# Five instead of four wide blocks, unsplit k and q projections, and a later plan for DMA results in a fused attention and feed-forward kernel

## Chip, cores and metric

The kernel runs on one core of one Trainium2 chip. Its time is device time in microseconds (us); 1131.34 us is the median of three runs (1127.63 to 1132.11). TensorE is called PE here, VectorE DVE, ScalarE ACT, GpSimd POOL; SP issues the DMAs.

## What is computed

Eight batches of eight heads, 576 tokens of 64 numbers each, go through a linear attention with a feature map; its output, seen as 4608 tokens of 512 numbers, goes through a two-layer network with a GELU.

```python
def phi(x):                                   # w_phi: 64 x 128
    proj = einsum('bhsd,df->bhsf', x, w_phi)
    proj = proj - max(abs(proj), axis=-1, keepdims=True)
    return concatenate([exp(proj), exp(-proj)], axis=-1)
q_p, k_p = phi(q), phi(k)
kv  = einsum('bhsf,bhsd->bhfd', k_p, v)
z   = sum(k_p, axis=2)
num = einsum('bhsf,bhfd->bhsd', q_p, kv)
den = einsum('bhsf,bhf->bhs', q_p, z)[..., None] + 1e-06
x   = (num / den) as 4608 x 512
h   = x @ w_in                                # 512 x 2048
g   = 0.5 * h * (1 + erf(h / sqrt(2)))
out = g @ w_out                               # 2048 x 512
```

## The kernel before

**Order.** The program does not run in the order in which it is written. Every operation is first recorded with an engine, an assumed cost and a rank (`op`, line 91). `Plan.order` (line 118) then replays all of them: on each engine it takes, among those whose inputs and buffers are there, the one with the lowest rank, and `emit` writes the instructions in the order of the starts found. Each engine then runs its own list strictly in that order, so an instruction that waits holds up all that stand behind it on its engine. The numbers from line 901 on are the planner's settings: `T0`, `T15`, `LEAD`, `ATR`, `TF` and `HOLD2` say when blocks and batches fall due, `WPACE` and `WSPAN` when weights do, `LUMP` and `LINGER` how much attention work is gathered before PE leaves the feed-forward products. What a DMA brings counts as usable at its planned landing (line 243).

**Attention, k side** (`k_quad`, line 395; 16 of them, two a batch). Four heads at a time. Keys `kt` stand with two heads on the two halves of the 128 rows. In nine chunks of 128 tokens they are multiplied by `w_phi` into `pk` (PSUM), DVE takes the absolute maximum `mx` and subtracts it into `ek`, ACT takes the two exponentials, and PE adds up `kv` (with a column of ones for the sums). For batches 0 and 1 (`b < EB`) each chunk is two fp32 products, one on each half of PE's rows. For batches 2 to 7 the way is "full": DVE splits `kt` into `kh` (a CAST to fp32r and a TENSOR_TENSOR for the rest), and three fp32r products with the block-diagonal weight `wbd` (128 x 256, two parts) make both heads at once.

**Attention, q side** (`q_pair`, line 503; 64 of them, a pair of heads and half of the tokens each). For batches 0 and 1 the queries `qt` are loaded with two heads on the row halves and multiplied in fp32, two products side by side. For batches 2 to 7 they are loaded twice over by two DMAs, DVE splits them into `qh` (CAST and TENSOR_TENSOR), and each head takes two fp32r products against `wd`. ACT copies `pq` to `pc`, POOL takes the maximum over partitions (`mb`), DVE subtracts, ACT takes two exponentials into `ef`; PE makes the numerators `pn`; DVE (`un`), POOL (`db`), DMAs through DRAM (`d_d`, `dc`, `r_d`) and a reciprocal on DVE make the quotients.

**Weights** arrive as 64-bit floats and are turned into two fp32r parts on ACT and DVE (`split_weight`, line 346; 32 of them, 5 DVE instructions each).

**Plain blocks** (`block`, line 620): 256 tokens each. DVE multiplies `xr` by the quotients and splits it (`xh`, `xl`). Eight units follow: 24 products of 128x256 into `ph`, two GELUs on ACT, `gl` on DVE, 12 products of 128x512 into `po`. Plain blocks run among the attention work.

**Wide blocks** (`wide_block`, line 718): 512 tokens each, with seven products instead of eight for the first layer (42 products of 128x256 a unit into `pa` and `pb`, 336 a block against 384 for two plain blocks). Their extra weight sums come from `combos` (line 688; `sw`, `sh` on DVE, written to DRAM). They use the buffers of the attention, so they wait for its end. `JW` = 5 makes ten plain blocks (0 to 9) and then four wide ones (5 to 8, counted in 512 tokens).

Of the kernel before, what the change touches and what calls it, by code (L numbers as in the profile page):

```python
# [285 lines left out]
def fused_kernel(ctx: ExitStack, tc: tile.TileContext, qT, kT, va, w_st, w_in, w_out, out):  # L286
# [108 lines left out]
    def k_quad(b, g, kvs, rank):  # L395
# [23 lines left out]
        for u, (p, cs) in enumerate(units):  # L419
# [22 lines left out]
            cols = slice(cs[0] * P, (cs[-1] + 1) * P)  # L442
            if way == "full":
                kh = sb["kh"]([P, 2, n * P], F32R, f"kh_{nm}_{u}")
                copy("dve", dve(n * P, fast=True), lambda kh=kh: kh()[:, 0], lambda cols=cols: kt()[:, cols], [kts[u]], [kh], also=[kt], **k())
# [3 lines left out]
                def proj(xb=xb, cs=cs, kh=kh):
                    ins = []  # L450
                    for i, c in enumerate(cs):
                        at = slice(i * 2 * NF, (i + 1) * 2 * NF)
# [50 lines left out]
    def q_pair(b, p, kvs, rank, halves=(0, 1)):  # L503
# [4 lines left out]
        for half in halves:  # L508
            nm = f"{b}_{p}_{half}"
            ss = slice(half * HS, half * HS + HS)  # L510
            qt = sb[("qt", "gh", "gl")[(2 * p + half) % 3] if b < EB else "qt"]([P, HS] if b < EB else [P, 2, HS], F32, f"qt_{nm}")
            if b < EB:
                op("sp", 0.06, lambda qt=qt, ss=ss: nc.sync.dma_start(out=qt(), in_=qT[b, p, :, ss]), w=[qt], kb=147, **k(1))
            else:
# [15 lines left out]
            if b < EB:  # L530
                op("pe", PAIR_Q, lambda of=of, qt=qt: [
                    mm(of[j](), lhsT=wst()[64 * j : 64 * j + 64], rhs=qt()[64 * j : 64 * j + 64], start=True, stop=True) for j in range(2)
                ], r=[qt, wst], w=pqs, also=[pc], kind="q", **k(1))
            else:
                for j in range(2):
# [444 lines left out]
```

## Time and profile before

| | |
|---|---|
| median of three runs | 1131.34 us |
| the profiled execution | 1126.56 us |
| its span, first to last instruction | 1124.8 us |
| PE busy | 1080.4 us (96%) |
| DVE busy | 760.1 us (68%) |
| ACT busy | 620.0 us (55%) |
| POOL busy | 328.2 us (29%) |
| mean granted TensorE clock | 0.993 |

The busy shares are means over stages that differ. A matmul is shown longer than the step to the next one, since matmuls overlap in the array: what one costs in a row of them is the difference of two starts. The rows below give the stages, the waits of PE and the costs of the single steps.

### The profile page before, as it was taken

How to read it: one execution, taken by the hardware profiler on the slowest of the kernel's cores; microseconds unless marked ns; L12 is line 12 of the kernel's file. 1: busy time of each engine (PE TensorE's matmuls, PEld its weight loads, DVE VectorE, ACT ScalarE, POOL GpSimd, SP SyncE). 2: the span in 40 equal slices, each digit the busy share in tenths (PEclk: the TensorE clock that was granted, in tenths of full speed). 3: DMA queues.
4: the chain of work that ended last, by engine and by line, in shares of the span. 5: the costliest groups of instructions: out<-in, count | busy, mean ns of one | idle time of the engine just before them, and what ended most of it. 6: DMA issues, size and time to landing. Idle time of an engine off the chain costs nothing.

```text
span 1124.8 us, 22298 instructions
## 1 busy us (share of the span) xinstructions
PE 1080.4 (96%) x8796; PEld 913.5 (81%) x8796; DVE 760.1 (68%) x1352; ACT 620.0 (55%) x1063; POOL 328.2 (29%) x116
## 2 busy tenths in 40 slices
PE   7887999998998999999999999999999999999998
PEld 5544887886887888888888888999898898888987
DVE  6998999678887999987778887223535535534332
ACT  5886786777776778778777643122223223222222
POOL 2153024445565656555466342000000000000000
PEclk9989999999999999999999999999999999999999
DMA  9965232333342342341322345502635534523421
GB/s 352 339 230 142 63 95 74 88 98 92 89 115 73 91 137 56 95 135 51 109 80 59 105 137 164 150 20 58 186 104 139 171 102 142 160 85 123 131 85 38
DMA packets 119480, 133.98 MB, mean 119 GB/s; under 512 B 28544, under 2 KB 88096, under 8 KB 119376
## 3 DMA queue, kind: packets, MB, share of 16 engines
q1 hardware_dynamic: 119376, 132.56, 39.6%
q8 instruction: 69, 1.13, 0.4%
q14 instruction: 35, 0.29, 0.1%
HBM read 104.96 MB, written 27.56 MB: 118 GB/s over the span
## 4 chain that ended last, share of the span: by engine, by line
PE 59%; DVE 21%; DMA 6%; ACT 4%; issue 4%; POOL 3%; SPq 2%; ACTq 0%; DVEq 0%; POOLq 0%
PE po L305 25%; PE ph L305 10%; PE pb L305 8%; PE pa L305 5%; PE pn L305 4%; PE kv L305 3%; POOL db L576 2%; PE pk L305 2%; DVE qh L331 2%; DVE pc L331 2%; PE pq L305 2%; DMA dc<-d_d 1%; DVE mx L469 1%; DVE qh L327 1%; DVE gl L331 1%
## 5 line engine op out<-in xcount | busy, mean ns | idle before, releaser
L305 PE MATMUL po<-w_o,gh 128*128 128x512 f32 x1152 | 362.1, 395 | 0.0
L305 PE MATMUL ph<-xh,w_i 128*128 128x256 f32 x1280 | 246.0, 281 | 1.5 <-DVE gl L331 1.5
L305 PEld LDWEIGHTS po<-w_o,gh 128*128 128x128 f32 x1152 | 205.6, 188 | 37.3 <-issue 0.4
L576 POOL PARTITION_ALL_REDUCE db<-un x48 | 178.3, 3714 | 178.5 <-DVE un L573 127.6
L305 PE MATMUL po<-w_o,gl 128*128 128x512 f32 x576 | 227.1, 394 | 0.0
L305 PEld LDWEIGHTS ph<-xh,w_i 128*128 128x128 f32 x1280 | 204.5, 188 | 5.9 <-issue 1.8
L541 POOL PARTITION_ALL_REDUCE mb<-pc x64 | 152.4, 2383 | 193.7 <-ACT pc L325 159.6
L305 PE MATMUL ph<-xl,w_i 128*128 128x256 f32 x640 | 181.0, 283 | 0.1
L305 PEld LDWEIGHTS po<-w_o,gl 128*128 128x128 f32 x576 | 108.3, 188 | 26.3 <-DVE gl L331 0.4
L305 PEld LDWEIGHTS ph<-xl,w_i 128*128 128x128 f32 x640 | 120.3, 188 | 2.2 <-DVE xl L331 0.4
L834 ACT ACTIVATE gh<-pa 128x512 fp32r<-128x512 f32 x32 | 19.2, 600 | 174.1 <-PE po L305 120.2
L305 PE MATMUL pn<-ef,kvn 128*64 128x288 f32 (+1 forms) x512 | 97.9, 423 | 10.8 <-ACT ef L547 7.4
L305 PEld LDWEIGHTS kv<-vt,ek 128*64 128x64 f32 (+1 forms) x2560 | 84.6, 139 | 28.8 <-issue 12.8
L547 ACT ACTIVATE ef<-pc 128x576 f32<-128x576 f32 x128 | 82.8, 679 | 29.9 <-DVE pc L331 29.2
L305 PE MATMUL kv<-vt,ek 128*64 128x65 f32 (+1 forms) x2560 | 94.0, 226 | 4.6 <-ACT ek L477 3.8
L477 ACT ACTIVATE ek<-ek 128x512 f32<-128x512 f32 (+1 forms) x140 | 82.0, 587 | 21.2 <-DVE ek L331 18.7
L331 DVE TENSOR_TENSOR gl<-ph,gh 128x512 fp32r<-128x512 f32 x80 | 54.9, 686 | 56.2 <-ACT ph L664 54.4
L663 ACT ACTIVATE gh<-ph 128x512 fp32r<-128x512 f32 x80 | 47.8, 598 | 80.7 <-PE ph L305 78.1
L305 PE MATMUL pb<-b,s 128*128 128x256 f32 x576 | 78.9, 282 | 1.0 <-DVE c L331 1.0
L305 PEld LDWEIGHTS pn<-ef,kvn 128*64 128x64 f32 (+1 forms) x512 | 38.8, 138 | 45.6 <-ACT ef L547 12.5
L305 PEld LDWEIGHTS pb<-b,s 128*128 128x128 f32 x576 | 73.0, 189 | 2.2 <-DVE c L331 1.6
L663 ACT ACT_TABLE_LOAD x57 | 73.1, 1283 | 1.9 <-PE ph L305 1.0
(84 smaller groups left out, 1558.3 us busy)
## 6 DMA issues: line engine op xcount, KB each, us to landing
s<-s_d SPq DMA_DIRECT2D x128, 256.0 KB
qt<-in_qT_dram SPq DMA_DIRECT2D x112, 144.0 KB
kt<-in_kT_dram SPq DMA_DIRECT2D x16, 576.0 KB
out_dram<-ob SPq DMA_DIRECT2D x36, 256.0 KB
raw_i<-in_w_in_dram SPq DMA_DIRECT2D x16, 512.0 KB
raw_o<-in_w_out_dram SPq DMA_DIRECT2D x16, 512.0 KB
x_d<-xo SPq DMA_DIRECT2D x48, 144.0 KB
vt<-in_va_dram SPq DMA_DIRECT2D x16, 325.0 KB
```

What stands on the lines that cost most here:

```text
L305: return tc.keep_in_program_order(nc.tensor.matmul(*a, **kw))
L327: op(eng, cost, lambda: e.tensor_copy(out=dst(), in_=src()), r=r, w=w, **kw)
L331: op(eng, cost, lambda: e.tensor_tensor(out=dst(), in0=a(), in1=b(), op=o), r=r, w=w, **kw)
L469: op("dve", dve(128 * n * nj, True), lambda view=view, mx=mx, js=js: nc.vector.tensor_reduce(out=mx()[:, 0].rearrange("p (j i) -> p j i", ...
L477: op("act", act(256 * n, inside), lambda at=at, es=es, s=s: nc.scalar.activation(es[s](), at(), AF.Exp, scale=1.0 - 2.0 * s), r=[parts[0][ ...
L541: op("pool", 2.2, lambda mb=mb, pc=pc: nc.gpsimd.partition_all_reduce(mb(), pc(), P, bass_isa.ReduceOp.absmax), r=[pc], w=[mb], **k(1))
L547: op("act", act(2 * HS), lambda ef=ef, pc=pc, s=s: nc.scalar.activation(ef()[:, s], pc(), AF.Exp, scale=1.0 - 2.0 * s), r=[pc], w=[ef], ta ...
L576: op("pool", 3.7, lambda db=db, un=un: nc.gpsimd.partition_all_reduce(db(), un(), P, bass_isa.ReduceOp.add), r=[un], w=[db], **k())
L663: op("act", act(2 * TB, True) + 0.016, lambda gh=gh, ph=ph: nc.scalar.activation(gh(), ph(), AF.Gelu), r=[ph], w=[gh], table="gelu", rank= ...
L834: op("act", act(2 * TB, psum) + 0.016, lambda gh=gh, at=at: nc.scalar.activation(gh(), at(), AF.Gelu), r=[at], w=[gh], table="gelu", rank= ...
```

## The change

One more pair of plain blocks becomes a wide one (`JW` = 4: plain blocks 0 to 7, wide blocks 4 to 8). For batches 2 to 7 the splits on DVE go. k is one unsplit fp32 product a chunk with an fp32 block-diagonal weight; q takes the way that batches 0 and 1 had, with one DMA instead of two. `wd` and `kh` are gone. A result of a DMA that another engine than PE reads is planned as there 4 us later (`LANDING`). The planner's settings are new.

```diff
+                u.ready = max(u.ready, ... 
+                              + (LANDING if o.eng == "sp" != u.eng and u.eng != "pe" and o.end > 130.0 else 0.0))
...
-    copy("dve", dve(NF), lambda: wd()[:, 0], wst, [wst], [wd], rank=-100.0)
-    tt("dve", dve(NF), lambda: wd()[:, 1], wst, lambda: wd()[:, 0].bitcast(F32), ALU.subtract, [wst, wd], [wd], rank=-100.0)
...
-    wbd = fixed([P, 2, 2 * NF], F32R, "wbd")
+    wbd = fixed([P, 2 * NF], F32, "wbd")
...
             if way == "full":
-                kh = sb["kh"]([P, 2, n * P], F32R, f"kh_{nm}_{u}")
-                copy("dve", dve(n * P, fast=True), lambda kh=kh: kh()[:, 0], lambda cols=cols: kt()[:, cols], [kts[u]], [kh], also=[kt], **k())
-                tt("dve", dve(n * P), lambda kh=kh: kh()[:, 1], lambda cols=cols: kt()[:, cols], lambda kh=kh: kh()[:, 0].bitcast(F32), ALU.subtract,
-                   [kts[u], kh], [kh], also=[kt], **k())
...
-                        for z, w in ((0, 0), (0, 1), (1, 0)):
-                            ins.append(mm(xb[0]()[:, at], lhsT=kh()[:, z, i * P : (i + 1) * P],
-                                          rhs=wbd()[:, w], start=len(ins) % 3 == 0, stop=len(ins) % 3 == 2))
...
+                    return [mm(xb[0]()[:, i * 2 * NF : (i + 1) * 2 * NF], lhsT=kt()[:, c * P : (c + 1) * P], rhs=wbd(), start=True, stop=True)
+                            for i, c in enumerate(cs)]
...
-                for i in range(2):
-                    op("sp", 0.06, lambda qt=qt, ss=ss, i=i: nc.sync.dma_start(
-                        out=qt()[64 * i : 64 * i + 64], in_=qT[b, p, :, ss].rearrange("(j d) t -> d j t", j=2)), w=[qt], kb=147, **k(1))
-                qh = sb["mb"]([P, 2, HS], F32R, f"qh_{nm}")
-                copy("dve", dve(2 * HS, fast=True), qh, qt, [qt], [qh], **k(1))
-                tt("dve", dve(2 * HS), lambda qh=qh: qh()[64:], lambda qt=qt: qt()[64:], lambda qh=qh: qh()[64:].bitcast(F32), ALU.subtract,
...
-                    op("pe", 2 * mm_cost(128, HS), lambda of=of, qh=qh, j=j: [
-                        mm(of[j](), lhsT=wd()[:, w], rhs=qh()[:, j], start=w == 0, stop=w == 1) for w in range(2)
-                    ], r=[qh, wd], w=[pqs[j]], also=[pc], kind="s", **k(1))
+            op("pe", PAIR_Q, lambda of=of, qt=qt: [
+                mm(of[j](), lhsT=wst()[64 * j : 64 * j + 64], rhs=qt()[64 * j : 64 * j + 64], start=True, stop=True) for j in range(2)
+            ], r=[qt, wst], w=pqs, also=[pc], kind="q", **k(1))
...
-JW = 5
+JW = 4
+LANDING = 4.0
-HOLD2 = 12.718
+HOLD2 = 73.438
-TF = 83.043
+TF = 65.043
-LUMP = 2.465
+LUMP = 1.394
-WPACE = 2.116
-WSPAN = 4.373
+WPACE = 2.884
+WSPAN = 12.477
-LEAD = 289.427
+LEAD = 316.642
-T0 = 76.06
+T0 = 83.683
```

DVE, ahead of the first plain block (`xl_0` is the last thing its first product needs; `wt` and `w` are weights). Before, at the place of `xl_0`; its partner `xh_0` stands 23 rows above it:

```order
L331 TENSOR_TENSOR w_i0_2_1437<-wt_i0_2_1348,w_i0_2_1437 128x512
L362 SCALAR_TENSOR_TENSOR wt_i1_2_1396<-raw_i1_2_509,wt_i1_2_1396 128x512
L331 TENSOR_TENSOR pc_1_3_1_1418<-pc_1_3_1_1418,mb_1_3_1_1435 128x576
L356 TENSOR_SCALAR wt_i2_2_1456<-wt_i2_2_1456 128x512
L331 TENSOR_TENSOR kh_2_0_1_1430<-kt_2_0_772,kh_2_0_1_1430 128x256
L331 TENSOR_TENSOR w_i1_2_1465<-wt_i1_2_1396,w_i1_2_1465 128x512
L358 TENSOR_SCALAR wt_i2_2_1456<-wt_i2_2_1456 128x512
L331 TENSOR_TENSOR xl_0_1485<-xr_0_1189,xh_0_1331 128x1024
```

And now:

```order
L330 TENSOR_TENSOR pc_1_3_0_1355<-pc_1_3_0_1355,mb_1_3_0_1372 128x576
L348 TENSOR_SCALAR wt_i0_2_1384<-wt_i0_2_1384 128x512
L326 CAST xh_0_1424<-xr_0_938 128x1024
L350 TENSOR_SCALAR wt_i0_2_1384<-wt_i0_2_1384 128x512
L330 TENSOR_TENSOR xl_0_1434<-xr_0_938,xh_0_1424 128x1024
L330 TENSOR_TENSOR w_o7_1436<-wt_o7_1300,w_o7_1436 128x512
```

`xl_0` has moved up to `xh_0`: work on weights `i0_2`, `i1_2` and `i2_2` that stood ahead of it stands behind it.

PE, in batch 4 (`pq_4_0_1` is the second half of its first pair of heads). Before, the two heads stand apart among products of plain block 3:

```order
L305 MATMUL ph_3_2_4287<-xh_3_3027,w_i3_1_1030 128x256
L305 MATMUL pq_4_0_1_0_4339<-qh_4_0_1_4300,wd_95 128x288 x2
L305 MATMUL po_3_4241<-w_o2_692,gh_3_1_4249 128x512 x2
L305 MATMUL po_3_4241<-w_o2_692,gl_3_1_4266 128x512
L305 MATMUL po_3_4241<-w_o2_692,gh_3_1_4249 128x512 x2
L305 MATMUL po_3_4241<-w_o2_692,gl_3_1_4266 128x512
L305 MATMUL pq_4_0_1_1_4355<-qh_4_0_1_4300,wd_95 128x288 x2
```

And now:

```order
L306 MATMUL ph_2_3_3688<-xh_2_2405,w_i3_1_1084 128x256
L306 MATMUL pk_4_1_2_3750<-wbd_80,kt_4_1_3115 128x256
L306 MATMUL pn_3_3_1_3754<-ef_3_3_1_3685,kvn_3_1_1_3200 64x288 x4
L306 MATMUL pq_4_0_1_0_3768<-qt_4_0_1_3719,wst_68 128x288
L306 MATMUL pq_4_0_1_1_3770<-qt_4_0_1_3719,wst_68 128x288
L306 MATMUL kv_4_1_0_3710<-vt_4_1_0_3528,ek_4_1_1_0_3701 64x65 x2
```

The two heads read `qt` as it was loaded, run side by side, and stand in one lump with other attention products; the block whose products stand around batch 4 is 2 instead of 3.

DVE, where the k side of batch 4 begins. Before:

```order
L327 CAST kh_4_0_0_3693<-kt_4_0_3025 128x256
L573 SCALAR_TENSOR_TENSOR un_3_1_1_3680<-ef_3_1_1_3567,kvn_3_0_1_3180,un_3_1_1_3680 128x288
L331 TENSOR_TENSOR kh_4_0_0_3693<-kt_4_0_3025,kh_4_0_0_3693 128x256
L573 SCALAR_TENSOR_TENSOR un_3_1_1_3680<-ef_3_1_1_3567,kvn_3_0_1_3180,un_3_1_1_3680 128x288
L327 CAST qh_3_2_1_3716<-qt_3_2_1_3613 128x576
L331 TENSOR_TENSOR qh_3_2_1_3716<-qt_3_2_1_3613,qh_3_2_1_3716 64x576
L469 TENSOR_REDUCE mx_4_0_0_3766<-pk_4_0_0_3749 128x4
L327 CAST kh_4_0_1_3782<-kt_4_0_3025 128x256
L331 TENSOR_TENSOR ek_4_0_0_0_3784<-pk_4_0_0_3749,mx_4_0_0_3766 128x512
L331 TENSOR_TENSOR kh_4_0_1_3782<-kt_4_0_3025,kh_4_0_1_3782 128x256
```

And now:

```order
L330 TENSOR_TENSOR gl_1_6_3088<-ph_1_6_3010,gh_1_6_3056 128x512
L451 TENSOR_REDUCE mx_3_1_4_3113<-pk_3_1_4_3107 128x4
L330 TENSOR_TENSOR ek_3_1_4_0_3128<-pk_3_1_4_3107,mx_3_1_4_3113 128x512
L451 TENSOR_REDUCE mx_4_0_0_3130<-pk_4_0_0_3110 128x4
L537 TENSOR_SCALAR un_3_0_1_3134<-ef_3_0_1_3105,kvn_3_0_0_2549 128x288
L330 TENSOR_TENSOR ek_4_0_0_0_3143<-pk_4_0_0_3110,mx_4_0_0_3130 128x512
```

The splits `kh` and `qh` are gone, and the maxima of batch 4 stand in plain block 1.

## Rows read from the trace of the kernel before

**Rows 1.** Stages: stretch, length, busy PE, PEld, DVE, ACT, POOL; clock, DMA share, GB/s.
```profile
0.00:115.20 115.20, 95.80 (x1024) 57.39 (x1025) 97.68 (x187) 84.86 (x184) 37.49 (x20) 0.94 0.77 260
115.20:697.70 582.50, 566.43 (x5170) 482.76 (x5168) 497.52 (x838) 423.64 (x673) 287.83 (x96) 1.00 0.34 95
697.70:768.60 70.90, 70.90 (x449) 63.58 (x446) 17.95 (x30) 14.91 (x28) 2.91 (x1) 1.00 0.30 82
768.60:1124.80 356.20, 347.25 (x2161) 309.73 (x2159) 146.96 (x298) 96.61 (x180) 0.00 (x0) 1.00 0.40 120
```

**Rows 2.** Waits of PE, 115.2 to 697.7 us: total us, times, longest.
```profile
PE pq L305 <- DVE qh L331: 8.5, 11, 1.5
PE pq L305 <- DVE ek L331: 2.6, 4, 1.6
...
PE ph L305 <- DVE gl L331: 1.5, 1, 1.5
```

**Rows 3.** PE in order of time: start us, us, instructions, [idle before <-releaser].
```profile
344.54 0.50 PE L305 MATMUL pq<-qh,wd 128*128 128x288 f32 x2 [1.54 <-DVE qh L331]
...
354.14 0.43 PE L305 MATMUL pq<-qh,wd 128*128 128x288 f32 x2
354.41 0.28 PE L305 MATMUL ph<-xh,w_i 128*128 128x256 f32 x1
```

**Rows 4.** DVE in order of time, at the same place.
```profile
343.43 0.18 DVE L596 TENSOR_SCALAR dc<-dc 128x18 f32<-128x18 f32 x1 [3.43 <-DMA dc<-d_d]
343.64 0.76 DVE L331 TENSOR_TENSOR qh<-qt,qh 64x576 fp32r<-64x576 f32 x1
```

**Rows 5.** Instructions by form, DVE: count, busy us, mean ns, idle before.
```profile
L331 DVE TENSOR_TENSOR qh<-qt,qh 64x576 fp32r<-64x576 f32 x48 | 49.0, 1022 | 1.6
L327 DVE CAST qh<-qt 128x576 fp32r<-128x576 f32 x48 | 41.4, 863 | 7.1 <-DMA qt<-in_qT_dram 5.7 <-PE ph L305 1.0 <-issue 0.3
L331 DVE TENSOR_TENSOR kh<-kt,kh 128x256 fp32r<-128x256 f32 x48 | 29.7, 619 | 0.4
L327 DVE CAST kh<-kt 128x256 fp32r<-128x256 f32 x48 | 24.6, 512 | 1.1 <-PE pk L305 1.0
```

**Rows 6.** PE in order of time, a k unit of two chunks and a kv group.
```profile
482.33 0.87 PE L305 MATMUL pk<-wbd,kh 128*128 128x256 f32 x6
483.03 0.27 PE L305 MATMUL ph<-xh,w_i 128*128 128x256 f32 x1
...
484.31 0.28 PE L305 MATMUL ph<-xh,w_i 128*128 128x256 f32 x1
484.52 0.68 PE L305 MATMUL kv<-vt,ek 64*64 64x65 f32 x16
```

**Rows 7.** PE in order of time, fp32 products of batches 0 and 1.
```profile
79.88 0.76 PE L305 MATMUL pq<-qt,wst 64*128 64x288 f32 x4
80.56 1.19 PE L305 MATMUL pn<-ef,kvn 128*65 128x288 f32 x4
81.68 0.68 PE L305 MATMUL kv<-vt,ek 64*64 64x65 f32 x16
```

**Rows 8.** Chain that ended last: start us, us, what; one unit of a plain block.
```profile
701.08 2.83 PE ph L305 x24
703.91 2.80 PE po L305 x12
```

**Rows 9.** PE in order of time, the last attention product and the first wide block's first.
```profile
696.89 1.19 PE L305 MATMUL pn<-ef,kvn 128*64 128x288 f32 x8
...
768.56 1.59 PE L305 MATMUL pb<-b,s 128*128 128x256 f32 x12
...
1120.01 0.40 PE L305 MATMUL po<-w_o,gl 128*128 128x512 f32 x1
```

**Rows 10.** DVE in order of time, ahead of the first plain block.
```profile
98.28 0.69 DVE L327 CAST xh<-xr 128x1024 fp32r<-128x1024 f32 x1
...
114.53 1.22 DVE L331 TENSOR_TENSOR xl<-xr,xh 128x1024 fp32r<-128x1024 f32 x1
```

More of the change, by code (lines that the diff above doesn't have):

```diff
@@ L242, in order @@
                 u.wait -= 1
-                u.ready = max(u.ready, o.end + o.late + (self.HOP if u.eng != o.eng else self.SAME)[o.eng] + (MARGIN if u.eng == "pe" != o.eng and o.end > 130.0 else 0.0))
+                u.ready = max(u.ready, o.end + o.late + (self.HOP if u.eng != o.eng else self.SAME)[o.eng] + (MARGIN if u.eng == "pe" != o.eng and o.end > 130.0 else 0.0)
+                              + (LANDING if o.eng == "sp" != u.eng and u.eng != "pe" and o.end > 130.0 else 0.0))
                 if u.wait == 0:
@@ L318, in fused_kernel @@
     op("sp", 0.06, lambda: nc.sync.dma_start(out=wst(), in_=w_st), w=[wst], kb=66, rank=-400.0)
-    wd = fixed([P, 2, NF], F32R, "wd")
     def copy(eng, cost, dst, src, r, w, **kw):
@@ L331, in tt @@
         op(eng, cost, lambda: e.tensor_tensor(out=dst(), in0=a(), in1=b(), op=o), r=r, w=w, **kw)
-    copy("dve", dve(NF), lambda: wd()[:, 0], wst, [wst], [wd], rank=-100.0)
-    tt("dve", dve(NF), lambda: wd()[:, 1], wst, lambda: wd()[:, 0].bitcast(F32), ALU.subtract, [wst, wd], [wd], rank=-100.0)
-    wbd = fixed([P, 2, 2 * NF], F32R, "wbd")
-    op("dve", dve(512, fast=True), lambda: nc.vector.memset(wbd().bitcast(F32), 0.0), w=[wbd], rank=WB)
+    wbd = fixed([P, 2 * NF], F32, "wbd")
+    op("dve", dve(2 * NF, fast=True), lambda: nc.vector.memset(wbd(), 0.0), w=[wbd], rank=WB)
     for j in range(2):
-        copy("dve", dve(2 * NF, fast=True), lambda j=j: wbd()[64 * j : 64 * j + 64, :, j * NF : (j + 1) * NF], lambda j=j: wd()[64 * j : 64 * j + 64],
-             [wd, wbd], [wbd], rank=WB)
+        copy("dve", dve(NF, fast=True), lambda j=j: wbd()[64 * j : 64 * j + 64, j * NF : (j + 1) * NF], lambda j=j: wst()[64 * j : 64 * j + 64],
+             [wst, wbd], [wbd], rank=WB)
     def split_weight(src, nm, rank):
@@ L441, in k_quad, with proj @@
             turn[0] += 1
-            cols = slice(cs[0] * P, (cs[-1] + 1) * P)
             if way == "full":
-                kh = sb["kh"]([P, 2, n * P], F32R, f"kh_{nm}_{u}")
-                copy("dve", dve(n * P, fast=True), lambda kh=kh: kh()[:, 0], lambda cols=cols: kt()[:, cols], [kts[u]], [kh], also=[kt], **k())
-                tt("dve", dve(n * P), lambda kh=kh: kh()[:, 1], lambda cols=cols: kt()[:, cols], lambda kh=kh: kh()[:, 0].bitcast(F32), ALU.subtract,
-                   [kts[u], kh], [kh], also=[kt], **k())
[L449 to L452, printed above, removed]
-                        for z, w in ((0, 0), (0, 1), (1, 0)):
-                            ins.append(mm(xb[0]()[:, at], lhsT=kh()[:, z, i * P : (i + 1) * P],
-                                          rhs=wbd()[:, w], start=len(ins) % 3 == 0, stop=len(ins) % 3 == 2))
-                    return ins
-                op("pe", 3 * n * mm_cost(128, 2 * NF), proj, r=[kh, wbd], w=xb, also=[mx, *e], kind="s", **k())
+                def proj(xb=xb, cs=cs):
+                    return [mm(xb[0]()[:, i * 2 * NF : (i + 1) * 2 * NF], lhsT=kt()[:, c * P : (c + 1) * P], rhs=wbd(), start=True, stop=True)
+                            for i, c in enumerate(cs)]
+                op("pe", n * FULL_K, proj, r=[kts[u], wbd], w=xb, also=[kt, mx, *e], kind="s", **k())
             else:
@@ L510, in q_pair @@
             ss = slice(half * HS, half * HS + HS)
[L511 to L514, printed above, removed]
-                for i in range(2):
-                    op("sp", 0.06, lambda qt=qt, ss=ss, i=i: nc.sync.dma_start(
-                        out=qt()[64 * i : 64 * i + 64], in_=qT[b, p, :, ss].rearrange("(j d) t -> d j t", j=2)), w=[qt], kb=147, **k(1))
-                qh = sb["mb"]([P, 2, HS], F32R, f"qh_{nm}")
-                copy("dve", dve(2 * HS, fast=True), qh, qt, [qt], [qh], **k(1))
-                tt("dve", dve(2 * HS), lambda qh=qh: qh()[64:], lambda qt=qt: qt()[64:], lambda qh=qh: qh()[64:].bitcast(F32), ALU.subtract,
-                   [qt, qh], [qh], **k(1))
+            qt = sb[("qt", "gh", "gl")[(2 * p + half) % 3] if b < EB else "qt"]([P, HS], F32, f"qt_{nm}")
+            op("sp", 0.06, lambda qt=qt, ss=ss: nc.sync.dma_start(out=qt(), in_=qT[b, p, :, ss]), w=[qt], kb=147, **k(1))
             pc = sb["pc"]([P, 2, HS], F32, f"pc_{nm}")
@@ L529, in q_pair @@
                 of = [lambda t=t: t() for t in pqs]
[L530 to L535, printed above, removed]
-                    op("pe", 2 * mm_cost(128, HS), lambda of=of, qh=qh, j=j: [
-                        mm(of[j](), lhsT=wd()[:, w], rhs=qh()[:, j], start=w == 0, stop=w == 1) for w in range(2)
-                    ], r=[qh, wd], w=[pqs[j]], also=[pc], kind="s", **k(1))
+            op("pe", PAIR_Q, lambda of=of, qt=qt: [
+                mm(of[j](), lhsT=wst()[64 * j : 64 * j + 64], rhs=qt()[64 * j : 64 * j + 64], start=True, stop=True) for j in range(2)
+            ], r=[qt, wst], w=pqs, also=[pc], kind="q", **k(1))
             for j in range(2):
@@ L909 @@
 GATE = 60
-T15 = 906.055
+T15 = 901.177
 BIAS = 40
 STICK = 2
-PATIENCE = 1.567
+PATIENCE = 0.947
 URGE = -1000.0
-EARLY = -18.706
-WPACE = 2.116
-WSPAN = 4.373
+EARLY = -26.856
+WPACE = 2.884
+WSPAN = 12.477
 WARM = 4
@@ L926 @@
 EPACE = 20.0
-TF = 83.043
+TF = 65.043
 ND = 2
-LUMP = 2.465
-LINGER = 3.999
+LUMP = 1.394
+LINGER = 4.006
 PAIR_K = 0.43
-PAIR_Q = 0.7
+FULL_K = 0.433
+PAIR_Q = 0.5
 PAIR_N = 1.18
@@ L935 @@
 PULL = -2000.0
-LEAD = 289.427
-HOLD = 44.655
-WR = -30.275
-ATR = -8.845
-T0 = 76.06
+LEAD = 316.642
+HOLD = 89.189
+WR = -14.66
+ATR = 9.181
+T0 = 83.683
 VERBOSE = False
```

2 lines of the change are left out of this document (1 added, 1 removed).

## Prediction

> **What bounds the kernel now.** I read the stages first [rows 1]. Up to 115.2 us PE is not the bound: it is busy for 95.8 us, with matmuls that are shown longer than the step they take, at a mean clock of 0.94 of 2.4 GHz, while DVE has 97.7 us of work. From 115.2 to 697.7 us, ten plain blocks and the attention of batches 2 to 7 share PE, which is idle for 16.1 of 582.5 us; but DVE is busy for 497.5 us (85%), ACT for 423.6 (73%), POOL for 287.8 (49%). Then come 71 us of plain blocks alone without a gap, and four wide blocks in 356.2 us, with DVE at 41%. So PE bounds all but the start, and what it loses in the middle is short waits. Who ends them [rows 2]: 8.5 us for the split queries `qh`, 2.6 us for `ek`, 1.5 us for a `gl`, all on DVE. One such place shows the mechanism: PE stands 1.54 us before `pq` [rows 3]; the subtraction that makes `qh` started only at 343.64 because the instruction ahead of it on DVE stood 3.43 us for the quotients' DMA [rows 4]. A shown wait hides some more, since a matmul is shown for 0.28 us or longer where the next follows after 0.12 [rows 3, 8]; with 0.16 us for each of some 20 waits, about 16 us are lost in this stage to DVE or through it.
>
> **Part 1, k without a split.** A unit of two chunks takes 0.70 us as six fp32r products (482.33 to 483.03), 0.35 a chunk [rows 6]. Now a chunk is one fp32 product of 128 rows by 256 columns. The trace of before has this only as `pn` of batches 0 and 1: two fp32 products of 288 columns in 1.12 us (80.56 to 81.68) [rows 7], so 0.56 each, and 0.50 if scaled to 256 columns. In that time lies a change of tile shape; one such change costs about 0.09 us on leaving (`ph` at 484.31 is followed after 0.21 instead of 0.12) [rows 6], and with some on entering I take off 0.13 for the two products: 0.44 a chunk. There are 12 quads of nine chunks: 108 x (0.44 - 0.35) = +9 us on PE. Bounds: +16 without taking anything off, +3 if a chunk in a lump with other attention work already costs 0.41 today, as 0.35 plus half a change.
>
> **Part 2, q on row halves.** So far a head is two fp32r products, 0.27 us (354.14 to 354.41) [rows 3], so 0.54 for a pair of heads. The pair in fp32 on the two halves takes 0.68 us from its start to that of the next group (79.88 to 80.56) [rows 7], with the change of shape behind it. That is +0.14 us, and up to 0.10 more where the change into it comes on top: 48 x 0.14 to 0.24 = +7 to +11.5. In the new order PE changes its tile shape 177 instead of 117 times behind the first `ph`, so the changes are not all shared; but most pairs stand beside `kv` or `pn`, which change the shape anyway. I take +8. The Trainium skill speaks against this part: "TensorEngine Tiling (Array Packing)", Key Properties, says that a change of tiling mode drains TensorE; the rows agree with about 0.1 us a change. The same page's table promises up to twice the speed for a contraction of 64; by that the pair would cost 0.27 us and the part would give 13 us back, which the 0.68 us of the row rule out here.
>
> **Part 3, the fifth wide block.** A unit of a plain block takes 2.83 + 2.80 us [rows 8], two blocks 90.1. Four wide blocks run from 768.56 to 1120.4 [rows 9], 88.0 each with their gaps. So -2 us; by the count alone, 48 products of 2.83/24 = 0.118 us fewer, it would be -5.7, the far bound.
>
> **Part 4, the waits.** `kh` and `qh` cost DVE 49.0 + 41.4 + 29.7 + 24.6 = 144.7 us [rows 5], more with the ninth chunks. The stage in the middle shrinks by two plain blocks, to some 490 us plus what parts 1 and 2 add; DVE then has at most 353 us of work in it, 72% or less. The split's own wait (8.5 us, and 11 times the hidden 0.16) goes entirely, since `qt` is now read as it lands; its DMA was loaded far ahead and, with one instead of two for each pair, stays so. Of the rest, planning DMA results 4 us later puts other work ahead of an instruction such as the one at 343.43, so I let half of it go. What is late next is the PSUM buffer of `pq`, freed by ACT and DVE. Sum: -14 of 16; bounds 0 and -18.
>
> **Part 5, the start.** The first plain product comes at 115.2, straight behind `xl` at 114.53, which stood 23 instructions behind `xh` at 98.28 [rows 10]. In the new order `xl` follows `xh` after one instruction. Counted with the mean duration of each form, 92.5 instead of 100.4 us of DVE work then stand up to and including `xl`, and PE has no less attention work before its first plain product. So -8 us; bounds -10 and 0, since weights are released more slowly and DVE could wait for their DMAs.
>
> **Free edits.** The three small instructions for `wd` (0.9 us) lie in the start beside DMAs. 48 DMA issues fewer for `qt` against 32 more for the sums of one more wide block: SP is never waited for in rows that end a PE wait.
>
> **Sum.** +9 + 8 - 2 - 14 - 8 = -7 us, and from about -24 to +26 if every part fell to the same end of its bounds. The profiled execution took 1126.56 us, 4.8 us less than the median of the runs shown; a change of some us is taken over unscaled, so the median should go from 1131.3 to about 1124.
>
> **Rivals.**
> (a) *Slower: ACT takes DVE's place.* ACT's work in the middle hardly shrinks (the attention's copies and exponentials stay), while the stage does: up to 424 us in 490, 86%, against 73%, and ACT also runs its list in order. If PE then waits for the copies of `pq` and for the GELUs as it did for DVE, part 4 gives nothing and the sum is +9 + 8 - 2 - 8 = +7; with the dearer q it is +11: 1138 to 1142. It decides when the average wait on ACT per q pair reaches 0.3 us (48 x 0.3 = 14 us). For it: [rows 1]. Against it: ACT ends almost none of PE's waits now, and PE's own work in the stage also falls more slowly than its length, so it stays the fullest.
> (b) *No change: gains and costs meet.* Half of the waits stay, or the first wide block comes late. Behind the last attention product there are now less than seven units of plain work, 6.9 x 5.63 = 39 us instead of 71 [rows 9], for the attention's last results to pass through DRAM and DVE to make the wide block's seven operands. Either costs some 6 us: 1127 to 1134.
> (c) *A larger gain.* Part 1 at its low bound, part 3 by the count, waits all gone: -7 - 6 - 4 - 4 = -21: about 1110.
> (d) *The change does not do what it says.* The later planned landing holds only for the planner; if the real landings are not what held DVE up, only the removed splits act: the half of "the rest" in part 4, 3 us, stays out: 1127.
>
> **How the numbers follow.** The forecast, 1124 us, has 0.45; (a) 0.18; (b) and (d) together 0.25; (c) 0.12. A measurement of this kernel can tell about 0.5% (5.7 us) from no change. The forecast's own spread, some 5 us either way, lies a little more than half on the faster side of 1125.7: 0.32 faster, 0.13 same. With (c) and a part of (b) and (d): faster 0.50; same 0.31; slower 0.19, from (a) and the edge of (b). The range reaches from (c) to (a), with a little beyond each: 1108 to 1141.
>
> **What would show it.** Right: no `pq` waits for DVE; a lower DVE share in the middle; the first plain product near 107 us; the unit of k at 0.85 to 0.95 us; the wide stage 88 us longer. Part 4 is wrong if PE's waits in the middle still come to over 10 us, and (a) is right if ACT ends them. Part 5 is wrong if the first product stays at 115. I am wrong altogether if the fp32 products cost PE much more than rows 7 suggest, or if PE waits over 5 us at the first wide block.

## The result and the profile after

The changed kernel takes 1112.75 us (median of four runs, 1111.32 to 1114.11) against 1130.38 for the kernel before on the same chip: ratio 0.985, 95% interval 0.982 to 0.987, so 17.6 us faster where 7 were forecast. One execution of all those below, one of run e12, took 2095.92 us and is left out of its median. The profiled execution took 1112.2 us with a span of 1110.4. These are its stages, to be read against [rows 1]; columns as there.

```profile
0.00:107.80 107.80, 93.36 (x1046) 59.68 (x1046) 90.10 (x175) 81.83 (x177) 33.55 (x19) 0.95 0.85 275
107.80:643.20 535.40, 530.23 (x4701) 429.49 (x4702) 356.68 (x617) 400.14 (x646) 284.29 (x97) 1.00 0.31 87
643.20:677.40 34.20, 34.20 (x221) 30.74 (x218) 11.92 (x22) 6.92 (x13) 0.00 (x0) 1.00 0.46 137
677.40:1110.40 433.00, 428.84 (x2678) 384.28 (x2676) 187.47 (x379) 120.62 (x224) 0.00 (x0) 1.00 0.42 126
```

In the second row DVE has fallen from 85% to 67% of the stage, ACT stands at 75%, and PE is idle for 5.2 us instead of 16.1. The longest waits of PE in this stage, against [rows 2] (total us, times, longest); none is for `qh`, and ACT ends most of what is left:

```profile
PE pk L306 <- ACT pc L324: 1.6, 3, 1.1
PE pq L306 <- DVE ek L330: 1.3, 1, 1.3
PE pn L306 <- ACT xo L324: 1.2, 3, 0.8
```

By three marks of the trace (first plain product, first wide product, end of the last product) the span divides so: up to the first mark 107.8 us instead of 115.2, -7.4; between the marks 569.6 instead of 653.4, which with the 90.1 us of two plain blocks fewer is +6.3; wide blocks 428.8 us for five instead of 351.8 for four, and +77.0 against 90.1 is -13.1. The forecast had -8, +3 and -2. The start and the middle came out near it, the middle in part by luck (see Part 4 below). The wide blocks did not, and they say where to look: in the kernel before they had waits of which the prediction showed no row.

```profile
DVE xr L331 <- DMA rp<-r_d: 19.1, 9, 4.3
...
PE pa L305 <- DVE u L331: 3.6, 3, 1.4
PE pb L305 <- DVE c L331: 1.0, 2, 0.6
```

These are waits of the kernel before, 768.6 to 1124.8 us. One of them in order of time, on DVE and then on PE (start us, us, instruction, [idle before <-releaser]):

```profile
879.52 0.68 DVE L331 TENSOR_TENSOR gl<-pa,gh 128x512 fp32r<-128x512 f32 x1
882.36 0.69 DVE L331 TENSOR_TENSOR xr<-xr,rp 128x512 f32<-128x512 f32 x1 [2.15 <-DMA rp<-r_d]
882.97 0.42 DVE L327 CAST b<-xr 128x512 fp32r<-128x512 f32 x1
883.31 0.69 DVE L331 TENSOR_TENSOR gl<-c,gh 128x512 fp32r<-128x512 f32 x1
883.91 0.41 DVE L331 TENSOR_TENSOR u<-u,pa 128x256 f32<-128x256 f32 x1
...
884.38 0.97 PE L305 MATMUL pa<-b,w_i 128*128 128x256 f32 x6 [0.89 <-DVE u L331]
```

DVE stands 2.15 us for the quotients `rp` of the *next* wide block. Behind that one instruction wait `gl` and `u` of the block that runs, and PE waits for `u`. After, again inside the second wide block, while the operands of the third are made, the multiplications stand further back, and the long wait is gone; the stage's total is 3.1 us in four waits, and PE shows none:

```profile
786.39 0.42 DVE L330 TENSOR_TENSOR u<-u,pa 128x256 f32<-128x256 f32 x1
786.73 0.69 DVE L330 TENSOR_TENSOR xr<-xr,rp 128x512 f32<-128x512 f32 x1
787.42 0.42 DVE L330 TENSOR_TENSOR u<-u,pb 128x256 f32<-128x256 f32 x1
...
788.75 0.69 DVE L330 TENSOR_TENSOR xr<-xr,rp 128x512 f32<-128x512 f32 x1 [0.45 <-DMA rp<-r_d]
...
DVE xr L330 <- DMA rp<-r_d: 3.1, 4, 1.4
```

### The profile page after: what moved, and what is told of

Same layout as the page of the kernel before. It is cut to its first block, busy times and chain, and to the rows that moved or that the text cites. A ratio compares the mean times of both kernels' runs of the same rounds, so it can differ in the third digit from the quotient of the medians.

```text
span 1110.4 us, 21848 instructions
## 1 busy us (share of the span) xinstructions
PE 1086.6 (98%) x8640; PEld 904.2 (81%) x8640; DVE 646.2 (58%) x1190; ACT 609.5 (55%) x1059; POOL 317.8 (29%) x116
## 4 chain that ended last, share of the span: by engine, by line
PE 79%; DVE 7%; ACT 5%; DMA 3%; issue 3%; POOL 1%; SPq 1%; ACTq 0%; DVEq 0%; POOLq 0%
PE po L306 33%; PE ph L306 13%; PE pb L306 10%; PE pa L306 8%; PE kv L306 5%; PE pn L306 4%; PE pk L306 4%; PE pq L306 3%; DMA raw_i<-in_w_in_dram 2%; POOL mb L508 1%; ACT L630 1%; ACT ek L459 1%; DVE mx L451 1%; ACT ef L514 1%; DVE ek L330 1%
## 5 line engine op out<-in xcount | busy, mean ns | idle before, releaser
L306 PE MATMUL ph<-xh,w_i 128*128 128x256 f32 x1024 | 201.6, 285 | 0.0
L306 PEld LDWEIGHTS ph<-xh,w_i 128*128 128x128 f32 x1024 | 165.0, 189 | 7.5 <-issue 3.9
L306 PE MATMUL ph<-xl,w_i 128*128 128x256 f32 x512 | 145.4, 284 | 0.0
L306 PEld LDWEIGHTS ph<-xl,w_i 128*128 128x128 f32 x512 | 96.9, 189 | 2.8
L306 PE MATMUL pb<-b,s 128*128 128x256 f32 x720 | 98.4, 282 | 0.0
L451 DVE TENSOR_REDUCE mx<-pk 128x4 f32<-128x512 f32 (+2 forms) x90 | 51.6, 577 | 73.6 <-PE pk L306 73.6
L306 PEld LDWEIGHTS pb<-b,s 128*128 128x128 f32 x720 | 91.5, 189 | 0.8
L330 DVE TENSOR_TENSOR gl<-ph,gh 128x512 fp32r<-128x512 f32 x64 | 44.0, 688 | 67.8 <-ACT ph L631 62.7
L306 PEld LDWEIGHTS pa<-b,w_i 128*128 128x128 f32 x480 | 67.4, 188 | 7.1
L537 DVE TENSOR_SCALAR un<-ef,kvn 128x288 f32<-128x288 f32 x96 | 49.5, 534 | 39.7 <-POOL db L543 37.0
```

The source lines that it names most:

```text
L306: return tc.keep_in_program_order(nc.tensor.matmul(*a, **kw))
L330: op(eng, cost, lambda: e.tensor_tensor(out=dst(), in0=a(), in1=b(), op=o), r=r, w=w, **kw)
L451: op("dve", dve(128 * n * nj, True), lambda view=view, mx=mx, js=js: nc.vector.tensor_reduce(out=mx()[:, 0].rearrange("p (j i) -> p j i", ...
L537: op("dve", dve(HS, fast=True) + 0.06, lambda un=un, ef=ef, one=one, j=j: nc.vector.tensor_scalar(out=un()[:, j], in0=ef()[:, 0, j], scala ...
```

## The experiments

The first theory was that the later plan (`LANDING`) took these waits out and that the rest came out about as forecast. Its rivals were the new settings and the fifth wide block. The table holds all runs, by what they are; the marks are us in each profiled span, the ratio is to the kernel before on the same chip.

| label | kernel | median us | ratio, 95% interval | first plain | first wide | last product ends |
|---|---|---|---|---|---|---|
| | before | 1130.38 | 1 | 115.2 | 768.6 | 1120.4 |
| | after | 1112.75 | 0.982 to 0.987 | 107.8 | 677.4 | 1106.2 |
| e2 | before, landing 4 | 1104.62 | 0.974 to 0.981 | 114.5 | 754.1 | 1098.7 |
| e11 | before, landing 4 in wide blocks only | 1121.18 | 0.990 to 0.995 | 113.8 | 769.4 | 1115.2 |
| e9 | e2, k unsplit | 1117.41 | 0.987 to 0.992 | 117.7 | 767.7 | 1113.6 |
| e10 | e2, q unsplit | 1114.22 | 0.983 to 0.989 | 111.5 | 761.0 | 1106.8 |
| e13 | e2, k and q unsplit | 1118.46 | 0.989 to 0.992 | 113.8 | 766.4 | 1112.1 |
| e14 | before, k and q unsplit | 1124.57 | 0.995 to 0.997 | 115.0 | 766.0 | 1118.2 |
| e3 | before, five wide | 1165.48 | 1.028 to 1.035 | 111.9 | 712.6 | 1159.5 |
| e8 | e2, five wide | 1161.57 | 1.028 to 1.032 | 113.7 | 719.6 | 1153.6 |
| e1 | after, landing 0 | 1127.68 | 0.997 to 1.002 | 109.1 | 676.8 | 1121.6 |
| e4 | after, four wide | 1115.95 | 0.984 to 0.991 | 107.9 | 765.0 | 1110.7 |
| e5 | after, k and q split | 1156.37 | 1.023 to 1.028 | 115.8 | 715.1 | 1148.3 |
| e6 | after, k split | 1140.37 | 1.009 to 1.013 | 109.1 | 699.5 | 1134.5 |
| e7 | after, q split | 1131.36 | 1.001 to 1.004 | 115.2 | 684.8 | 1120.4 |
| e12 | after, k and q split, four wide | 1124.52 | 0.994 to 0.998 | 117.9 | 773.1 | 1118.8 |
| e16 | before, landing 2 | 1115.55 | 0.987 to 0.990 | 114.3 | 762.9 | 1108.7 |
| e17 | before, landing 3 | 1112.72 | 0.982 to 0.988 | 114.7 | 759.4 | 1105.2 |
| e18 | before, landing 5 | 1110.26 | 0.981 to 0.985 | 113.4 | 755.4 | 1104.2 |
| e15 | before, landing 8 | 1160.76 | 1.027 to 1.030 | 115.4 | 800.8 | 1156.1 |

### The later plan, taken away, alone, and in one stage

```diff
-LANDING = 4.0
+LANDING = 0.0
```

> The changed kernel with LANDING = 0, all else kept (the planner counts a DMA result as there at its planned landing again). Theory (the extra gain is the wide stage's waits, removed by the later plan): the five wide blocks take 438 to 441 us instead of 428.8 (about 88 each), DVE waits again some 15 to 20 us for the quotients rp there with gl and u behind, and the time is about 1121 to 1125 us (9 to 12 us slower than the changed kernel's 1112.75). Rival 1 (the new settings and order made the wide stage smooth, landing is not it): wide stage stays within 2 us of 428.8, time 1111 to 1116. Rival 2 (a fifth wide block is itself the gain): the same as rival 1.

The wide blocks took 444.7 us instead of 428.8, and the gain of the whole change was gone. Waits of the wide stage, DVE's and PE's:

```profile
DVE xr L330 <- DMA rp<-r_d: 31.8, 11, 5.5
...
PE pa L306 <- DVE u L330: 8.1, 4, 2.8
```

This is the theory's mechanism. Its size was above the expectation (15.9 us in the stage against 9 to 12). The middle did not get longer (567.7 us against 569.6): with the splits gone, the later plan is worth nothing there.

```diff
+                              + (LANDING if o.eng == "sp" != u.eng and u.eng != "pe" and o.end > 130.0 else 0.0))
...
+LANDING = 4.0
```

> The kernel before with the later plan alone (LANDING = 4 in the planner's line, its other settings kept). Theory: the wide stage's waits go, four wide blocks take about 343 us instead of 351.8, and some of the middle's waits for the split queries go too: 1130.4 - 9 to - 13 = 1117 to 1121 us. Rival 1 (the settings): no change, 1127 to 1134, with rp waits of DVE still 15 us or more. My prediction's own term for it, half of the middle's other waits, would give -3: 1127.

The kernel before with this line alone, all splits and four wide blocks kept, is faster than the changed kernel: 1104.62 us, an interval of the ratio that ends below that of the changed kernel. Theory and rival had both set the gain too low. The wide stage gives 7.2 us of the 8.8 expected; another 14 lie in the middle. There DVE waited for DMAs in the kernel before (first three lines, 115.2 to 697.7 us), and hardly with the later plan (next two, 115 to 750); most of PE's waits for the split `qh` went with them (last line, against 8.5 in [rows 2]):

```profile
DVE dc L596 <- DMA dc<-d_d: 13.0, 9, 3.4
DVE qh L327 <- DMA qt<-in_qT_dram: 5.7, 4, 3.3
DVE xr L331 <- DMA xr<-x_d: 2.7, 2, 1.7
```
```profile
DVE qh L328 <- DMA qt<-in_qT_dram: 1.6, 2, 0.9
DVE dc L597 <- DMA dc<-d_d: 0.4, 1, 0.4
...
PE pq L306 <- DVE qh L332: 1.5, 2, 0.8
```

```diff
-u.eng != "pe" and o.end > 130.0 else 0.0))
+u.eng != "pe" and u.names else 0.0))      # names: recorded by a wide block
```

> The kernel before with the later plan only for instructions of the wide blocks; the attention and the plain blocks are planned as before. Theory: the wide stage's 7 us come back (344.6 instead of 351.8), the middle keeps its waits (about 653 between first plain and first wide product): 1121 to 1125 us; the other 14 us of the later plan lie in the middle. Rival (the wide blocks' multiplications are what stands in the way everywhere, or a later plan shifts all): 1104 to 1112, or no change, 1128 to 1132.

As the theory had it: 345.8 us of wide blocks, a middle of 655.6 with its 9.2 us of `qh` waits, 1121.18 us. So of the later plan's gain about 6 to 7 us lie in the wide blocks and 14 to 16 in the middle.

### The unsplit projections

The edits are those of the diff, one at a time, with the costs that the planner assumes for the new products (`FULL_K`, `PAIR_Q`), on the kernel before with `LANDING` = 4.

> The kernel before with LANDING = 4 (1104.6 us) and the unsplit k projection alone; four wide blocks, settings of before. Theory (with the later plan the waits are gone, so the unsplit product is only dearer on PE): part 1's +9, so 1111 to 1116 us, all of it between the first plain product and the first wide one. Rival (fewer instructions on DVE shorten waits also here): 1100 to 1107.

> The kernel before with LANDING = 4 (1104.6 us) and the unsplit q projection on row halves alone. Theory: part 2's +8, so 1110 to 1116 us; with the 2.1 us of qh waits that stand in that kernel taken off, 1108 to 1114. Rival: 1099 to 1106.

> The kernel before with LANDING = 4 and both projections unsplit; four wide blocks, settings of before. With the later plan alone it was 1104.6, with k unsplit too 1117.4 (+12.8), with q unsplit too 1114.2 (+9.6). Theory (each is a price on PE, and both add up): 1125 to 1129 us. Rival (together they relieve DVE enough to give some back): 1108 to 1118, near the changed kernel's settings with four wide blocks (1115.95).

Each makes that kernel slower, k by 12.8 us and q by 9.6, and both by 13.8: q as expected, k a little over it, and the sum well under. The windows from first plain to first wide product tell why (columns as in [rows 1]; kernels e2, e9, e10 and e13 in this order):

```profile
114.40:754.00 639.60, 634.90 (x5626) 547.96 (x5625) 503.44 (x863) 449.44 (x708) 284.73 (x96) 1.00 0.34 96
```
```profile
117.70:767.70 650.00, 640.02 (x5433) 547.11 (x5432) 459.68 (x740) 433.61 (x690) 286.80 (x96) 0.99 0.34 95
```
```profile
111.50:761.00 649.50, 645.00 (x5627) 536.67 (x5626) 434.69 (x775) 455.24 (x717) 287.90 (x97) 1.00 0.29 83
```
```profile
113.80:766.30 652.50, 649.76 (x5464) 537.65 (x5463) 372.38 (x654) 440.61 (x702) 283.21 (x96) 1.00 0.30 83
```

PE's busy time rises by 5.1 us for k, 10.1 for q and 14.9 for both. That these add up says little, since the windows don't hold the same work: ahead of the first plain product stand 1023, 1098, 1013 and 1067 products. Over the whole span PE's busy time rises by 13.3, 10.2 and 15.9 us, so the price of q is firm and that of k is not. PE's idle time in the windows, length less busy, is 4.7, 10.0, 4.5 and 2.7 us. With k alone, half of what this stretch loses is new waits (for `qh` 4.1 us instead of 1.5, and 2.7 for one `gh`); with both edits they go. Why k alone brings them is open.

> The kernel before with both projections unsplit and nothing else: no later plan, four wide blocks, settings of before. My prediction's parts 1, 2 and 4 together gave +9 + 8 - 14 = +3: 1133. Theory (the later plan and the missing splits cure the same waits of the middle; without the plan the wide stage keeps its 7 us): 1128 to 1136 us, waits of PE in the middle under 8 us. Rival (without the later plan the dearer products are not covered at all): 1140 to 1150.

Without the later plan the same two edits are a gain, 4.9 us, and more than expected. PE's idle time in the middle falls from 16.1 to 2.2 us (first line), so the missing splits cure what the later plan cured, and pay for it with dearer products. The wide blocks keep their waits (second line) and take 352.2 us:

```profile
115.00:766.00 651.00, 648.85 (x5465) 535.91 (x5464) 383.92 (x654) 432.56 (x695) 285.73 (x96) 1.00 0.29 83
...
PE pa L305 <- DVE u L331: 4.1, 3, 1.4
```

### Four or five wide blocks

```diff
-JW = 5
+JW = 4
```

> The kernel before with JW = 4 alone: five wide blocks. My prediction's part 3: 88.0 for 90.1 us, -2 us: 1128, if the attention still ends at the same distance. Rival 2 (the fifth wide block brings much more, 90.1 - 85.8 and better): 1120 to 1124 with wide blocks of about 86 us. A third outcome: without the later settings the first wide block waits for the attention's end, 1130 to 1140, with PE idle over 5 us ahead of the first wide product.

> The kernel before with the later plan and five wide blocks (LANDING = 4, JW = 4), its projections and settings kept. If the fifth wide block is worth what two plain blocks less one wide one give (90.1 - 86.1 us): 1104.6 - 4 = 1100 us. Rival (with the settings of before the attention ends too late for it: with JW = 4 alone PE waited 25 us for b ahead of the first wide product): the attention ends at 715 us and the plain blocks at about 664, so the first wide block comes 20 to 30 us late: 1120 to 1135.

> The changed kernel with JW = 5, all else kept: ten plain blocks and four wide ones. If a wide block costs 85.8 us here and two plain ones 90.1, it is 4.3 us slower: about 1117. Theory: the four wide blocks take 343 us (85.8 each). Rival 2 (the fifth block is the gain): 1122 to 1126.

> The changed kernel with the split k and q projections of the kernel before (kh, qh, wd back), its LANDING, its five wide blocks and its settings kept. Theory (the later plan already takes the waits for the splits away, so that the unsplit products are only dearer on PE, +9 for k and +8 for q as in parts 1 and 2): 17 us faster than the changed kernel, 1094 to 1099 us; stretch from the first plain product to the first wide one about 553 us instead of 569.6, DVE busier by some 145 us there with hardly a wait of PE for qh. Rival (the gain of the unsplit products is real and only their waits matter; settings were laid out for them): PE waits for qh again 8 us or more and the time is 1110 to 1118.

> The changed kernel with the split k projection of the kernel before, and the unsplit q. Theory: part 1 alone back, 108 chunks at 0.35 instead of 0.44 us: 1112.75 - 9 = 1103 to 1105 us. Rival (waits for kh, or DVE the fuller one): 1110 to 1116.

> The changed kernel with the split q projection of the kernel before (two DMAs, qh, four products a pair), and the unsplit k. Theory: part 2 alone back, 48 pairs at 0.14 to 0.24 us less: 1112.75 - 8 = 1102 to 1107 us. Rival (the split's wait comes back): PE waits for qh 5 us or more, 1110 to 1118.

> The changed kernel's settings and LANDING with the split projections and four wide blocks: with JW = 4 PE waited 26.8 us for b ahead of the first wide product, since the attention ended at 693 us. Theory (the unsplit products pay only by ending the attention early enough for the fifth wide block): with four wide blocks this wait is gone and the time is that of the kernel before with the later plan, 1104.6, less what the changed start brings (0 to 7 us): 1097 to 1106 us, under the changed kernel's 1112.75. Rival (the new settings don't suit the split products, whatever the wide blocks): 1115 to 1130, with PE waits of over 10 us in the middle.

Runs e3, e8 and e4 have this edit alone, e4 in the other direction; e5, e6 and e7 give the changed kernel its splits back, and e12 is e5 with four wide blocks. In the changed kernel the fifth wide block is worth 3.2 us by the medians and 4.5 by the marks (e4), not quite clear of noise: the intervals of e4 and of the changed kernel overlap. The four wide blocks of e4 took 345.7 us, where 343 were expected. Elsewhere it costs 37 us (e3 against before), 57 us (e8 against e2) and 32 us (e5 against e12): the third outcome of e3 and the rival of e8, each above its price. I had expected split projections in the changed kernel to make it 17 us faster (e5); it became 44 us slower, and e6 and e7 fell the same way, by 28 and 19 us. Kernel e5 shows what happens, PE and then DVE in order of time:

```profile
687.98 0.39 PE L306 MATMUL po<-w_o,gl 128*128 128x512 f32 x1
691.53 2.19 PE L306 MATMUL pn<-ef,kvn 128*64 128x288 f32 x8 [3.16 <-ACT ef L548]
715.12 1.21 PE L306 MATMUL pa<-b,w_i 128*128 128x256 f32 x2 [21.41 <-DVE b L328]
```
```profile
694.29 0.94 DVE L574 SCALAR_TENSOR_TENSOR un<-ef,kvn,un 128x288 f32<-128x288 f32 x2
701.72 0.18 DVE L597 TENSOR_SCALAR dc<-dc 128x18 f32<-128x18 f32 x1 [6.49 <-DMA dc<-d_d]
701.93 0.27 DVE L598 RECIPROCAL dc<-dc 128x18 f32<-128x18 f32 x1
712.90 0.69 DVE L332 TENSOR_TENSOR xr<-xr,rp 128x512 f32<-128x512 f32 x1 [10.70 <-DMA xr<-x_d]
...
714.55 0.42 DVE L328 CAST b<-xr 128x512 fp32r<-128x512 f32 x1
```

The plain blocks run out at 688, the attention's last `pn` comes at 691.5, and its results pass through two DMA round trips before the wide block's first operand `b` is made at 714.6, 23 us later. In the changed kernel the same way takes 22.7 us, but 34 us of plain products stand beside it:

```profile
642.42 1.19 PE L306 MATMUL pn<-ef,kvn 128*64 128x288 f32 x8
...
677.39 0.87 PE L306 MATMUL pa<-b,w_i 128*128 128x256 f32 x6
```
```profile
665.09 0.42 DVE L326 CAST b<-xr 128x512 fp32r<-128x512 f32 x1
```

So with four plain pairs the attention has to end by about 654 us (677 less 23; a rough mark, since the same way took 16 us in e7 and 30 in e6), and it does so only with both splits gone: its last product is at 693 us with both splits (e5), 669 with either (e6, e7), 643 with none. PE's waits for `b` come to 26.8, 25.9 and 11.1 us in e5, e6 and e7; e7 also starts 7.4 us later than the changed kernel. With four wide blocks this wait is gone, and e12 still takes 1124.52 us, its rival's figure. It differs from e2 in the settings alone, and 15.6 of the 20 us between them lie in the middle. PE loses much of that right behind the start, 108 to 200 us, where it is busy for 80.6 us against 89.3 in e2 (e12, then e4, the same without splits):

```profile
108.00:200.00 92.00, 80.61 (x602) 64.87 (x602) 87.10 (x155) 66.77 (x112) 29.62 (x10) 0.93 0.27 73
```
```profile
108.00:200.00 92.00, 90.20 (x832) 73.64 (x831) 82.89 (x144) 77.58 (x130) 33.20 (x12) 0.98 0.32 86
```

602 products instead of 832, at a granted clock of 0.93 instead of 0.98. DVE is busy for 87 of 92 us, but in e2 it is for 86.3 there, and PE makes 738 products. So a full DVE alone does not explain it. That the new settings do not suit the splits is shown; which setting does it, and by what, was not tried.

### How late a landing should be planned

The number behind `LANDING` is the only edit.

> The kernel before with LANDING = 2. DVE stood up to 4.3 us for the quotients before, 2.1 us a time on average. Theory (the gain grows with the share of landings covered): between both, 1108 to 1120 us. Rival (any shift of the order does it): 1102 to 1107.

> The kernel before with LANDING = 3. Measured so far: 0 gives 1129, 2 gives 1115.6, 4 gives 1104.6, 8 gives 1160.8. Theory (the gain grows with the share of landings covered, whose waits were up to 4.3 us): 1106 to 1114 us. Rival (each value gives another order by chance, 4 is a lucky one): outside of 1104 to 1116.

> The kernel before with LANDING = 5. Theory (4 us covers what is to be covered, a little more costs little until the attention ends later than the plain blocks): 1102 to 1115 us. Rival (the attention's end moves past the plain blocks already here, as with 8): 1130 or more, with PE waiting for b ahead of the first wide product.

> The kernel before with LANDING = 8 instead of 4 on the planner's line. Theory (4 us covers most landings; rp is waited for 2.0 us at one place and PE for 5 to 6 us in all): 1102 to 1106 us, the same as with 4. Rival (the later, the better): 1095 to 1101. A third outcome (results lie unused, buffers are held longer): 1108 or more.

With 0, 2, 3, 4, 5 and 8 us the kernel before takes 1129, 1115.6, 1112.7, 1104.6, 1110.3 and 1160.8 us. It is a slope and a cliff. From 115 to 697.7 us DVE's waits for all DMAs shrink as the landing grows (22.9, 8.6, 7.0, 1.6, 0.4 us and none), and up to 5 PE's idle time between its first plain and first wide product with them (16.1, 12.3, 8.2, 4.7 and 2.7 us). From 4 on the last attention product comes later: 698, 682, 672, 716, 725 and 779 us. The rivals of e16 and e17, by which any other order would do or 4 be a lucky one, did not come at their figures; the theory of e15, that 8 does no harm, failed. At 8 the last attention product is behind the last plain one at 758.6, and PE waits as in e5:

```profile
PE pa L306 <- DVE b L328: 32.4, 2, 21.4
```

That 4 beats 5 by 5.6 us is partly the same: at 5 PE waits 2.9 us for `b`, and its granted clock is 0.52 and 0.50 just behind (763 to 767 and 767 to 770 us), where six products `pa` take 1.28 us instead of 0.72. The rest I leave open. From 3 to 4 the kernel gains 8 us while PE's idle time falls by 3.5, so some luck in the order at 4 is not ruled out.

## Why the prediction was right or wrong

- **Part 1, k, +9:** on PE +5.1 us of work in the middle and +13.3 in all (e9), 5.6 on top of q (e13 against e10): inside the bounds of +3 to +16, with no firmer figure. One unit of two chunks starts at 406.67 in e9, the second product behind it at 407.65; less one step of 0.12 that is 0.86 us against 0.70, in the band named; 54 units at 0.16 would be +8.6, an estimate from these two rows.

```profile
406.67 1.03 PE L306 MATMUL pk<-wbd,kt 128*128 128x256 f32 x4
407.35 0.47 PE L306 MATMUL ph<-xh,w_i 128*128 128x256 f32 x1
407.65 0.28 PE L306 MATMUL ph<-xl,w_i 128*128 128x256 f32 x1
```

- **Part 2, q, +8:** +10.1 us (e10), 0.21 for each of 48 pairs, inside 0.14 to 0.24. Pairs in fp32 on the row halves stay dearer than the split, as the rows of batches 0 and 1 said. The 0.27 us that the prediction set against this halved the split's 0.54; the fitting comparison is two fp32 products one after the other, 1.12 us as `pn` in [rows 7], against 0.68 side by side.
- **Part 4, the waits of the middle, -14:** PE's idle time there falls by 13.9 us (16.1 to 2.2) when the splits alone go (e14). The size is right, and so is the mechanism for the split's own waits. The 3 us that the part gave to the later plan went without it, and taking the plan away brought none of them back (e1). With parts 1 and 2 this makes -2.4 us in e14's middle, where +3 was said. The +6.3 of the changed kernel is near that +3 in part by luck: from e13, at -0.8, the settings added 4.5 (e4) and the fifth wide block 2.6.
- **Part 5, the start, -8:** the first plain product came at 107.8, 7.4 us earlier. But e13 and e4, which differ in the settings (and two small `wd` instructions at the start, which e13 keeps), reach the first wide product at 766.4 and 765.0 although their first plain products are 5.9 us apart. The step took an earlier start for an earlier end; the middle gave 4.5 us of it back.
- **Part 3, the wide blocks, -2:** the term that failed: -13.1 were measured. It priced a wide block at the 88.0 us at which four ran, waits included, and counted only what the fifth adds. The waits for `rp` stood in the first three of the four (the last has no next block to prepare), and they went: 351.8 to 345.7 us (e4), -6.1. The fifth then added 83.1 us to the stage for 90.1 of plain blocks, -7.0, a little beyond the far bound of -5.7; the middle took 2.6 of it back. The sign that the prediction named, a wide stage 88 us longer, came as 77.0. Part 4 looked for waits only up to 697.7 us; PE's own waits in the wide stage, 4.6 us as shown, were read past, and so was DVE's line of 19.1 us.
- **Rivals.** (d), that the later plan changes nothing real, fell: it is the largest single gain, 24 us alone. I had given it 3 us. (a) did not come, ACT ends 3 to 4 us of PE's waits after. Its 86% took the stage for 490 us, though the prediction itself left 39 us of plain work behind the attention instead of 71, which makes some 522; the stage took 535.4, with ACT at 75%. (b) is right in its mechanism, the first wide block that comes too late, in e3, e5, e6, e7, e8 and e15: PE waits 11.1 us for `b` in e7 and 26 to 34 in the others, and where runs can be set against each other it costs 32 to 57 us rather than 6; the changed kernel keeps clear of it by about 12 us. (c) gave about the time that came, 1110, but by other terms: k at its low bound is not shown, and nearly half of what the wide blocks gained was their waits, which it did not hold either.
- **The sum.** By the end of the last product: 1120.4 before; 1118.2 with unsplit projections (e14); 1112.1 with the later plan too (e13); 1110.7 with the new settings (e4); 1106.2 with the fifth wide block: -2.2, -6.1, -1.4 and -4.5, in all -14.2. The remaining 3 us between that and -17.6 lie mostly in the profiled execution of before, which was 3.8 us faster than its median. In another order the same steps read otherwise: the later plan first is -21.7, the unsplit projections then +13.5. The change contains two cures for one wait, and pays for the second.

The version that beats both is e2: the kernel before with the later plan alone.

## What to carry to other kernels

Where each engine runs a fixed list, look at every instruction that waits for a DMA and at what is queued behind it: moving such instructions back in the plan was worth more here than taking work off the waiting engine. Two edits against the same wait are to be priced each with the other in place, since the second may buy nothing there and still cost, as here. And a stage's own waits belong into the price of one of its blocks before blocks are exchanged.
